# A block-sparse attention and gated-MLP kernel: the sign of the float64 weights carried by a parametric ReLU's slope instead of a 16-bit write on ScalarE, with the order of work searched anew

## The chip, the cores and the metric

The kernel runs on one core of a Trainium2 chip. The metric is the device time of one execution in microseconds (us); before the change it is 959.79 us, the median of 3 runs (959.57 to 961.75).

## The reference, cut to what matters

The reference is a strided sparse attention (8 batches, 8 heads, 576 positions, 64 per head) whose output, 4608 tokens of 512 values, goes through an RMS norm and a gated MLP of width 1536.

```python
scores = where(mask, q @ k.T / sqrt(64), -1e9)       # local or strided mask, by head
attn   = softmax(scores) @ v
x      = attn as (4608, 512)
xn     = x / sqrt(mean(x * x) + 1e-6) * rms_g
out    = (silu(xn @ w_gate) * (xn @ w_val)) @ w_out  # (512, 1536), (512, 1536), (1536, 512)
```

The weights come to the chip as float64, 18.9 MB in all, and the engines have no such type. So the kernel makes float32 words out of the 64-bit words itself, and then splits each float32 into a high and a low part that TensorE multiplies in its single-pass float32 format (fp32r), three products for one.

## The kernel before, in words

**Stages.** The 4608 tokens are 9 chunks of 512. Chunk 0 is computed plainly (three products per block: high by high, low by high, high by low): for each of 12 units of 128 hidden columns `slot_g`, `gemm1` and `slot_o` make the gate, the value and the output product. The other eight chunks are computed in four pairs (`pair_of_chunks`), each pair with seven block products in place of eight, on combinations of the weights. The 32 units of attention (`unit_s`: scores and softmax; `unit_o`: values) are spread over this: four before the first product, eight during chunk 0, the others during the pairs.

**Conversion of the weights** (`convert_weights`, 18 calls, done during the start and chunk 0). A call loads 1 MB of float64 into four slots of SBUF (L1007, SP's queue). Each 64-bit word is two 32-bit cells, cell 0 the low one and cell 1 the high one. The first call is done in two halves, so each operation below comes 17 times with 1024 elements a partition and twice with 512.

- L1006, ScalarE: cell 1, read as float32, is multiplied in place by 2 to the power of -112, which moves the float64 exponent to where a shift by three bits leaves a float32 exponent.
- L1011, ScalarE: byte 3 of cell 0 (its top eight bits) becomes its top three bits as a number, written as a 16-bit integer into the low half of cell 0.
- L1014, ScalarE: cell 1 is converted to a 16-bit float and written into the high half of cell 0. The value is so small that only its sign bit is left, at bit 31 of cell 0.
- L1015, VectorE: cell 1 is shifted left by three (which drops its sign) and combined with cell 0 by a bitwise or; the result is the float32 word.
- `pair_split`: L973 (VectorE) subtracts the high parts; the high parts themselves are casts by `copy_to` (L594 on ScalarE or L596 on VectorE, as the planner chooses).
- L1020, SP's queue: the float32 words are stored to `wd`. The high and low parts are stored to `gvd` and `od` (L1028). During the first pair, `words_of` (L1042) loads the words again, `TLEAD` units ahead, `transform_gv` and `transform_o` combine them, and the results are stored too.

**What sets the order.** `Plan.op` records each operation with its cost and its dependencies; `Plan.forward` then lays them out on the engines by a table of due times (`DUE`), and picks ScalarE or VectorE for the operations that may run on either. `PLACE` is a table of the SBUF slots. Each engine then runs its queue in that order. The planner's price for a ScalarE operation on n elements is

```python
return SLOWER * ((55 if psum else 95) + n / 1.2 + 70 * (n > CH))
```

in ns, with `SLOWER` 1.0 and `CH` 512, so 1018 for 1024 elements; L1011 is priced at 120 more.

Of the kernel before, what the change touches and what calls it, by code (L numbers as in the profile page):

```python
# [11 lines left out]
F32 = mybir.dt.float32  # L12
# [69 lines left out]
TLEAD = 1  # L82
# [5 lines left out]
    "0020140e0412081c2e102c24554e46593d00201856424a4c0e221257403a4d4b5030414852280e2c2614221006181e0c0408241832140626305c5838"  # L88
    "001a04343e3637531328202e020834002c3b445451461c10020e475430493f143224302812300c5b43393b55080604183c5d58453c1c2c2e0e142226"
    "1a403951465c2800020c4b4f554919081032181c34240e3e58405d5a4b0a422a47085c534f5a2e38301e39523f5b2942484c371e395c153c4b58003b"  # L90
    "3d2a554d283a3e400341012b4f161a040a180c104a5a2c32512f59235653141f092e2608191d1a385443321b575a5630202d4e5047381c5905331c14"
    "161024020e44501a54194e43224a3834045a1d530d190f2f3336591e300824510f0c1d340413444e104a3516205a5319440f1319302c114336143208"
    "242d0e0c4e3012021e5316320451180e311e0c100c2c255a172e1424084a1912140e0c1f180211431832202d15533019512c5a06152e1024054a2f32"
    "2e51212207515333271f2f4a04085b2b0b520a0937293d13103a43123f2d014b024c03515c4d113b402a2500285a27585319524a374a3e2c26083c2b"
    "074248242041050b220a2a513b43252d5506394b095c023f03532101194c2328372940045a58112c12543c374d28083e484a07425b50424f26330656"
    "13250a24222a204b571039232b5041383d32003b595b21373f58545c272812095a55150311160b533a054e403c2c51024d4204014f2d362943313044"
    "4746330715081c4b4a0c183e583d2730433f31372a471a4c0a46301849561d1c5c59074b1513580614343b4c43174a325a1a4525183d48331b4b0016"
    "26322831220d5b5c3b093019063f08485414374607120f591735323f2549451455313d1f483f0c0a141e1614314c3b5d5a144717244318585c553e56"
    "265c22444a37450a182548490f0c095b4c5921431347445a3b075d43145d064a08303f59002754455b285624205c4a580a312a26595b2506480c1858"
    "445c48565845123025284556455a3d5310134a032c4e2b38390b07313e21510120024c3b09572d3f115441084f5c4a535a04222a5010402b4d004e2c"  # L100
    "360b5b4259533039073d05203b44515c2858134c2309030a4e4f06123c480122103e04064d2d213a2912025a2b1137382a554333383f57205031130b"
    "36583d05463b00083c3039425c4147535d2c4c4d2d0a54064b2348075b030d553a24563528291001511f431d091c2a1204401e4921343e5922443711"
    "2038023f194115271336500c252617474b441a592b2d1652064d192e3433233e0d2c4c3d0c1722371350260f321a20244d4b5236020c5a50335d530f"
    "3e593807163f474d0e224f572f115805164b5c2d524e5b342f0a4e3d37502c4e5824314f33531b384406324c2d54595d485c4f1b15152152575c4b3e"
    "075d02502f444138034c5825534e2225543d0c34262f23245952214e4c41440b152b3e0c32372652371326054b3e48203d1507502721574e5359265c"
    "5a374c24150658354609521155030a083b0251542234441c40390456310b42013c491d3e4b24262b283d2a523b1157292b0921102346003a0706501e"
    "50200405511f433e540239341e0a5a310355303d2653355810291c4c1208133c210b5c0e595c372f0b4e0d425141501f46362e055b44232240024807"
    "4f560a011d09203e2d572c291c59353b5d4d3c12492b154c210c4b08111343310442003406102a3928523a5803541e555a3053360b14372f0f463d27"
    "16050f0e573d4a19592c510e123f1a5b413824253c23373b1a50323e142e1c453d1b3b5930542c204a1d5c2e4d325a4e1f190345370d47361b595746"
    "5d3f3518091b380e470b273305490c2f17192255234a5b5147410f3d1c3b2c472d265a472720372f4e3d3f182b4a1e270903530d57375c174915124a"  # L110
    "3546055b3d53443f3b500b324e4d3c16383d0e474d0c490f3615224a29192c2b145b0e5d0915533c380e301e0d03181412511d1c231f205a07130b35"
    "4d4744282d4e42110548570206364f403b0817501c4b0b074c04431d492913582312105c2c3d572022484a534256211f1e2b520a390509024d583c4b"
    "0051131d4e3a340111435b5a2830315518362a0b033221351252572d45381c3d2c2b06475129091d5c2f4408403b23485d2a0d4429"))
DUE = np.frombuffer(bytes.fromhex(
    "01600c6e018201990d7d0d94017600010026000c01f80d970002017a00030000001201a6000e00050058019f005c003c00370038006200ad00ef0028"
    "00480178005d00b600dc0118005603ca00ce0462004d0023002c000b00060015001c000a00180d9601be0096009700870008006600a0017200ba017c"
    "0014004400530035002b000d087d014000eb0122011f015c01ad00360034004600570042003b001a0004002a012b0116010f01ca010c01f9000900c4"
    "009a00fc008b006d00b0012904ce005a0063002900a6013300e30221013700f502a702c0013e0007008c00670064011b0185035401a303d101f602e3"
    "01cc0010002e0055005900410032002400bd010a019c00a7008f006500e20039003d00210114026401e601250095004a01570086015f011a015802d8"
    "0195019002a4013c018701ba0d9200b300b1005b030c016e052100bc014a01eb012e01770132015901170130018a013800f000ca00cd00a1015001cb"  # L120
    "016600c801c7019701a4024c01930183004e002d00130098007500a5010d01910b52016f009e007400400043001e0161023b0219015a02330201016d"
    "00f301c00027005f000f00f401df025101c30d430051020c00b902c80336011e0d930151012a0243002000f8018c014d014f02d9030a019801bb00bf"
    "016800d8006b00d900b200f9011201e8019d01ab0101020a008201d401bd02550226023a01e104f10030021100ea00f700de015500cb021600b50175"
    "0135008d0147013d0c3601a2001f02670214010b00ff02170124027a022b00d1008a00aa007a007d01a0011d012f01e701b30184016a012d021b0259"
    "024d023502c5001d00df00e000e90153014e0050007f0052007c0099020b012702ee0248023f0144026b0263026e03cc00a2041a026a01e502f70180"
    "02ce009c003e007900db010000b70094025c020f0212025801f70207021d01c60272026d02aa0296020902e1043102f6016b02c90289029b02340283"
    "04070318001700af013405e600d402080077010700a4016c029e00d000d501090928028c025e029202a300bb00e4027e01f501f301a8013f005400b8"
    "02280277018f0271027d031902360262028e01b701e302b801ea01ef02bc0241011901dc009b010500e5007600a900d6007304c6029302ac001603db"
    "02b9002202030222021302c402a202b1025702370239018e019a017b02ab021c01e4027903230297026001d801f1028b0294022e033a025d032d02b5"
    "01f402e9019b03ce025a02af035502820316025304090374020201c901cd022d022402de0210027301b2022002b302bb01fa02a002870245020001d1"  # L130
    "0254028a02e502cd02c30256029502d30232023d017d029d02ea01e202be03fa01ff024a02e0027f0335024602f20420033c035c027801c501fb0261"
    "02440230028d018601fc02850252022a02d2018d03200174024e022701b0030102fc01cf029902dd02ae045b02a601c402750173016202a502f9025b"
    "053802fd029c02470194025f01bf024f036e02400333034b036603bf018b022c021a0231020401fe026602ca01d601d902d4012c01a502a1022f0165"
    "010401b6020e03c103fb02f402d0035e031d02c7023c0154014801810171021f02d1026f02e40307031c02ff032402bf041801da023e0341029a02f8"
    "0163015d028105dc01db01a700fa00a302b603260313022300fb034002bd034d037b02c2033102fa00e80084014b0192017900f20268030602150276"
    "0205027001210309017e00c6038704c1037002cb0047004b00110329037c02d5039f031103f3013101de02d601b902ec02f101ec01e902a902d7032c"
    "0115020601a901360164028402e60070030e040500c700f10090006802ad0451031001d0027b01bc030001d302cc02c6028f034a03c2033701aa0381"
    "021e02f5045f03490286020d01e0039e0120034f02ed02b2038902dc0238038500dd028003530347024b038302ef001903320348032f034e0d95032b"
    "001b0377044e026c01d702e7029f035903aa02ba038801ce03a102b703b0036102cf037e0141037803b3038c0473009105470304032a007801ed03df"
    "02b402db00a803b4042503a002e803ad03ba0576030202df039a01d50156036802e202da04900582032e039b0265036903b2035003710330036c0314"  # L140
    "03b1030d04710412015b0363027404ba031a0169031701670434038a038d037a03fd042a0327038403ef035f03c0041c04b803ac037303dd040a03ab"
# [301 lines left out]
def attn_moe(ctx: ExitStack, tc: tile.TileContext, qz: bass.AP, qT: bass.AP, kT: bass.AP, vz: bass.AP, vl: bass.AP,  # L443
             wgv: bass.AP, wo: bass.AP, gain: bass.AP, consts: bass.AP, out: bass.AP):
    nc = tc.nc
# [124 lines left out]
    def act(n, psum=False):  # L570
        return SLOWER * ((55 if psum else 95) + n / 1.2 + 70 * (n > CH))
# [107 lines left out]
    def unit_s(i):  # L679
# [43 lines left out]
        if quick:  # L723
# [21 lines left out]
            if i not in HALFQ:  # L745
                op("ACT", 9 * 295, 0, exps, reads=keys_ + [sk], writes=pkeys + [sk], tab="exp")
# [916 lines left out]
```

## Time and profile before

| | |
|---|---|
| median of 3 runs | 959.79 us (959.57 to 961.75) |
| the profiled execution's own time | 959.39 us |
| its span, first to last instruction | 957.6 us |
| PE (TensorE) busy | 908.5 us, 95% |
| VectorE (DVE) busy | 723.1 us, 76% |
| ScalarE (ACT) busy | 602.0 us, 63% |
| mean granted TensorE clock | 0.974 |
| DMA | 234.26 MB, mean 245 GB/s |

Shares of the whole span hide stages with different limits. The view of the span in slices shows where each engine is full, the table by stretches gives the same in us for the stages named above, the groups by line give the duration of one instruction, and the views of waits tell what ended an engine's idle time. A group's busy time counts overlapping instructions of the group once.

### The profile page before, as it was taken

To read this page: it belongs to the slowest core of one execution; us is meant where nothing else is said; L and a number is where in the kernel's file an instruction comes from. 1 tells how busy PE (TensorE), PEld (TensorE's weight loads), DVE (VectorE), ACT (ScalarE), POOL (GpSimd) and SP (SyncE) were. 2 spreads that over 40 slices of the span, in tenths; PEclk is the share of its full clock that TensorE was granted. 3 is DMA by queue.
4 is the path that set the end of the run, shared out by engine and by line. 5 is a ranking of instruction groups with operands and counts; after the bars stand their busy time and mean duration, and the time that the engine had idled before them with its cause. 6 is when DMAs were issued, how large, how long until landed. Compare 5 with 4: busy or idle time off the path is not lost.

```text
span 957.6 us, 20822 instructions
## 1 busy us (share of the span) xinstructions
PE 908.5 (95%) x8295; PEld 726.0 (76%) x8295; DVE 723.1 (76%) x1222; ACT 602.0 (63%) x1178; POOL 1.2 (0%) x12
## 2 busy tenths in 40 slices
PE   6877778799999999999999999999999999999998
PEld 4555566577877888788887788888888888888886
DVE  5666777699988999966766999845579994356992
ACT  6999999976778787544645775444546923333430
POOL 0000000000000000000000000000000000000000
PEclk9877989999999999999999999999999999999999
DMA  9976988669998885598754756985436588543751
GB/s 358 355 265 211 357 294 316 224 213 376 396 394 297 304 308 189 171 366 280 232 170 125 252 181 218 343 278 179 120 99 226 190 302 303 189 138 117 230 154 66
DMA packets 104513, 234.26 MB, mean 245 GB/s; under 512 B 11616, under 2 KB 13920, under 8 KB 102112
## 3 DMA queue, kind: packets, MB, share of 16 engines
q1 hardware_dynamic: 103696, 232.34, 70.6%
q8 instruction: 65, 1.06, 0.4%
q10 hardware_dynamic: 720, 0.59, 0.2%
q14 instruction: 32, 0.26, 0.1%
HBM read 180.98 MB, written 51.90 MB: 243 GB/s over the span
## 4 chain that ended last, share of the span: by engine, by line
PE 59%; DVE 1%; DMA 0%; issue 0%; ACT 0%
PE a L1254 16%; PE g L1254 10%; PE v L1254 10%; PE a L1407 8%; PE g L1407 6%; PE v L1407 6%; PE pair L712 1%; PE pair L797 1%; PE a L797 1%; DMA out_dram<-bl 0%; DVE bl L602 0%; DVE bl L908 0%; PE pair L899 0%; DVE bl L596 0%; ACT bl L594 0%
## 5 line engine op out<-in xcount | busy, mean ns | idle before, releaser
L1254 PE MATMUL a<-bl,bl 128*128 128x512 f32 x857 | 217.0, 394 | 0.8 <-ACT bl L1262 0.7
L1254 PEld LDWEIGHTS a<-bl,bl 128*128 128x128 f32 x857 | 158.3, 188 | 36.3 <-ACT bl L1262 1.1
L594 ACT CAST bl<-bl 128x512 fp32r<-128x512 f32 (+1 forms) x203 | 124.1, 646 | 72.4 <-DVE bl L1210 28.8
L602 DVE TENSOR_TENSOR bl<-bl,bl 128x512 fp32r<-128x512 f32 x244 | 160.7, 686 | 9.6 <-ACT bl L594 4.6
L1254 PE MATMUL g<-bl,bl 128*128 128x512 f32 x564 | 145.6, 391 | 0.7 <-DVE bl L1292 0.7
L1254 PE MATMUL v<-bl,bl 128*128 128x512 f32 x566 | 145.1, 390 | 0.0
L1210 DVE TENSOR_TENSOR bl<-bl,bl 128x512 f32<-128x512 f32 x168 | 114.2, 687 | 40.1 <-ACT bl L1271 37.9
L1254 PEld LDWEIGHTS g<-bl,bl 128*128 128x128 f32 x564 | 105.3, 188 | 24.8 <-DVE bl L1292 2.2
L1254 PEld LDWEIGHTS v<-bl,bl 128*128 128x128 f32 x566 | 105.9, 188 | 22.8 <-DVE bl L1292 0.3
L1266 DVE TENSOR_TENSOR a<-a,bl 128x512 f32<-128x512 f32 x96 | 66.7, 696 | 62.5 <-PE a L1254 52.1
L1407 PE MATMUL a<-bl,bl 128*128 128x512 f32 x420 | 99.0, 391 | 0.1
L1407 PEld LDWEIGHTS a<-bl,bl 128*128 128x128 f32 x420 | 78.5, 188 | 17.4 <-DVE bl L596 0.5
L1407 PE MATMUL g<-bl,bl 128*128 128x512 f32 x282 | 67.2, 390 | 0.0
L1407 PE MATMUL v<-bl,bl 128*128 128x512 f32 x282 | 66.9, 389 | 0.0
L1271 ACT ACTIVATE bl<-a 128x512 f32<-128x512 f32 x48 | 28.8, 600 | 55.5 <-DVE a L1266 53.2
L1407 PEld LDWEIGHTS v<-bl,bl 128*128 128x128 f32 x282 | 52.9, 188 | 11.1 <-ACT bl L1271 0.2
L1407 PEld LDWEIGHTS g<-bl,bl 128*128 128x128 f32 x282 | 52.8, 188 | 11.2
L1262 ACT COPY bl<-g 128x512 f32<-128x512 f32 x48 | 28.2, 588 | 51.4 <-PE g L1254 49.8
L1262 ACT COPY bl<-v 128x512 f32<-128x512 f32 x48 | 28.2, 588 | 49.5 <-PE v L1254 48.8
L596 DVE CAST bl<-bl 128x512 fp32r<-128x512 f32 (+1 forms) x95 | 40.8, 442 | 12.0 <-PE v L1254 6.5
L1100 PE MATMUL g<-bl,bl 128*128 128x512 f32 x120 | 38.0, 456 | 11.2 <-DVE bl L596 5.2
L1011 ACT ACTIVATE bl<-bl,few 128x1024 uint16<-128x1024 uint8 (+1 forms) x19 | 47.7, 2512 | 0.0
(166 smaller groups left out, 1244.0 us busy)
## 6 DMA issues: line engine op xcount, KB each, us to landing
bl<-gvd SPq DMA_DIRECT2D x288, 256.0 KB, 4.5
bl<-od SPq DMA_DIRECT2D x168, 256.0 KB, 3.5
gvd<-bl SPq DMA_DIRECT2D x12, 1024.0 KB, 8.0
bl<-in_wgv_dram SPq DMA_DIRECT2D x11, 1024.0 KB, 8.5
wd<-bl SPq DMA_DIRECT2D x18, 512.0 KB, 6.9
bl<-wd SPq DMA_DIRECT2D x18, 512.0 KB, 7.0
vt<-in_vl_dram SPq DMA_DIRECT2D x24, 352.0 KB, 5.3
xk<-in_kT_dram SPq DMA_DIRECT2D x28, 288.0 KB, 5.5
```

What stands on the lines that cost most here:

```text
L594: nc.scalar.copy(out=o, in_=i)
L596: nc.vector.tensor_copy(out=o, in_=i)
L602: elementwise(CH, lambda e: both(e).tensor_tensor(out=lo.new(F32R), in0=src(), in1=hi.f32(), op=ALU.subtract), reads + [hi.key], [lo.key])
L797: nc.tensor.matmul(out=ends[r % 2][0][n][64 * h:64 * h + 64, at + 32 * lo:at + 32 * hi], lhsT=va()[32 * r:32 * r + 32, D * (6 * n + j):D * ...
L1011: op("ACT", act(n) + 120, 0, lambda cell=cell, half=half, w_=w_: nc.scalar.activation(out=half(0), in_=wide(raw_, U32)[:, w_].bitcast(mybi ...
L1100: nc.tensor.matmul(out=out_, lhsT=q.t[:, w + at:w + at + P], rhs=x.t, start=(kc == 0 and i == 0), stop=(kc == KC - 1 and i == 2))
L1210: elementwise(CH, lambda e: both(e).tensor_tensor(out=o.new() if fresh else o.t, in0=a.t, in1=b.t, op=how), [a.key, b.key], [o.key])
L1254: nc.tensor.matmul(out=banks[bk], lhsT=w, rhs=xs[k][y].t, start=start and k == 0 and i == 0, stop=stop and k == 1 and i == 2, skip_group_c ...
L1262: op("ACT", act(CH, True), 0, lambda: nc.scalar.copy(out=t.new(), in_=banks[bk]), reads=[bk], writes=[t.key])
L1266: op("DVE", dve(CH), 0, lambda: nc.vector.tensor_tensor(out=banks[bk], in0=banks[bk], in1=t.t, op=ALU.add), reads=[t.key], writes=[bk])
L1271: op("ACT", act(CH, True), 0, lambda: nc.scalar.activation(out=t.new(), in_=banks[bk], func=AF.Silu), reads=[bk], writes=[t.key], tab="silu")
L1407: nc.tensor.matmul(out=banks[bks[j]], lhsT=v, rhs=xs[k][y].t, start=start and k == 0 and i == 0, stop=stop and k == KT - 1 and i == 2, ski ...
```

## The change

The sign bit no longer needs an operation of its own. L1006 (L1003 after the change) becomes a parametric ReLU: a positive value is multiplied by 2 to the power of -112 as before, a negative one also by the slope, 2 to the power of 32. That adds 32 to the eight bits of the exponent, and the shift by three in the VectorE operation moves just this bit to the sign's place. L1011 (L1008 after) writes its three bits as a 32-bit integer over the whole of cell 0. L1014 goes. All line numbers behind it are 4 lower after the change.

```diff
-TLEAD = 1
+TLEAD = 2
...
-    "0020140e0412081c2e102c24554e46593d00201856424a4c0e221257403a4d4b5030414852280e2c2614221006181e0c0408241832140626305c5838"
...
+    "080c18281c16242c2e003402513f303a4908120456054c4110220f46204e3d43361e5a45501826200c1422322a18100034080634181c12300e405324"
...
-                op("ACT", 9 * 295, 0, exps, reads=keys_ + [sk], writes=pkeys + [sk], tab="exp")
+                op("ACT", 9 * 290, 0, exps, reads=keys_ + [sk], writes=pkeys + [sk], tab="exp")
...
-                op("ACT", 9 * 300, 0, rows, reads=[sk], writes=pkeys + [sk], tab="exp")
+                op("ACT", 9 * 333, 0, rows, reads=[sk], writes=pkeys + [sk], tab="exp")
...
-            def half(t, w_=w_):
-                return wide(raw_, U32)[:, w_].bitcast(mybir.dt.uint16).rearrange("p (n t) -> p n t", t=4)[:, :, t]
-
             def scale(cell=cell):
                 h = cell(1).bitcast(F32)
-                nc.scalar.activation(out=h, in_=h, func=AF.Copy, scale=2.0 ** -112)
+                nc.scalar.activation(out=h, in_=h, func=AF.Prelu, scale=2.0 ** -112, alpha=2.0 ** 32)
...
-            op("ACT", act(n) + 120, 0, lambda cell=cell, half=half, w_=w_: nc.scalar.activation(
-                out=half(0), in_=wide(raw_, U32)[:, w_].bitcast(mybir.dt.uint8).rearrange("p (n t) -> p n t", t=8)[:, :, 3],
+            op("ACT", act(n) + 120, 0, lambda cell=cell, w_=w_: nc.scalar.activation(
+                out=cell(0), in_=wide(raw_, U32)[:, w_].bitcast(mybir.dt.uint8).rearrange("p (n t) -> p n t", t=8)[:, :, 3],
                 func=AF.Identity, scale=1.0 / 32, bias=low3), reads=["low3"], writes=wk + [("wq", 1)])
-            op("ACT", act(n), 0, lambda cell=cell, half=half: nc.scalar.copy(out=half(1).bitcast(mybir.dt.float16), in_=cell(1).bitcast(F32)), writes=wk + [("wq", 2)])
```

`PLACE` and `DUE` are new tables throughout, so nearly every instruction may stand elsewhere in its queue, and in other slots. The two costs of 9 exponentials (L746, L758) are prices of the planner and no work.

ScalarE's queue in chunk 0, at one place of the conversions (L757 and L743 are the nine exponentials of an attention unit, L1121 the Silu of a unit of chunk 0, `few` holds constants). Before:

```order
L1006 ACTIVATE bl_145<-bl_145 128x1024
L1011 ACTIVATE bl_145<-bl_145,few 128x1024
L1014 CAST bl_145<-bl_145 128x1024
L1006 ACTIVATE bl_402<-bl_402 128x1024
L757 ACTIVATE pp_69,st_76<-pp_69,st_76 128x64 x9
L594 CAST bl_1485<-bl_1238 128x512
L1121 ACT_TABLE_LOAD
L1121 ACTIVATE bl_484<-bl_484 128x512
L1011 ACTIVATE bl_402<-bl_402,few 128x1024
L1014 CAST bl_402<-bl_402 128x1024
```

After, the same stretch of the queue:

```order
L1003 ACTIVATE bl_155<-bl_155 128x1024
L1008 ACTIVATE bl_155<-bl_155,few 128x1024
L757 ACTIVATE pp_69,st_76<-pp_69,st_76 128x64 x9
L1117 ACT_TABLE_LOAD
L1117 ACTIVATE bl_1467<-bl_1467 128x512
L1003 ACTIVATE bl_129<-bl_129 128x1024
L1008 ACTIVATE bl_129<-bl_129,few 128x1024
L878 ACTIVATE bl_1556<-bl_744 128x512
L594 CAST bl_810<-bl_132 128x2x256
L594 COPY bl_535<-pair 128x288
```

Two instructions stand for three in a conversion, no table load stands ahead of L1003, and a square (L878), a high-part cast and an evacuation of attention stand here. Up to the twelfth Silu of chunk 0, ScalarE's queue has 18 table loads after the change and 17 before.

VectorE's queue at the same place. Before:

```order
L753 TENSOR_REDUCE st_76<-pp_69 128x9
L1015 SCALAR_TENSOR_TENSOR bl_579<-bl_145 128x1024
L602 TENSOR_TENSOR bl_1467<-bl_970,bl_1136 128x512
L596 CAST bl_1474<-bl_579 128x2x256
L596 CAST bl_844<-bl_579 128x2x256
L973 TENSOR_TENSOR bl_1474<-bl_579,bl_1474 128x2x256
L1120 TENSOR_TENSOR bl_484<-g,bl_656 128x512
```

After:

```order
L753 TENSOR_REDUCE st_76<-pp_69 128x9
L1011 SCALAR_TENSOR_TENSOR bl_132<-bl_155 128x1024
L1116 TENSOR_TENSOR bl_1467<-g,bl_643 128x512
L596 CAST bl_776<-bl_132 128x2x256
L973 TENSOR_TENSOR bl_673<-bl_140,bl_673 128x2x256
L973 TENSOR_TENSOR bl_776<-bl_132,bl_776 128x2x256
```

The operation that makes the words keeps its place among the softmax steps; one of the two high-part casts has gone to ScalarE. Up to the twelfth multiplication of gate and value (L1137 before, L1133 after), VectorE's queue has 7 copies (L596 COPY), 3 high-part casts (L596 CAST) and 4 squares (L880) fewer.

## Rows read from the trace of the kernel before

**Rows 1.** The page's busy times in 40 slices of 23.9 us each.

```profile
PE   6877778799999999999999999999999999999998
ACT  6999999976778787544645775444546923333430
PEclk9877989999999999999999999999999999999999
DMA  9976988669998885598754756985436588543751
```

**Rows 2.** Busy time by stretches: start, chunk 0, its end, first pair, rest.

```profile
core 0: us, PE busy (x) PEld busy (x) DVE busy (x) ACT busy (x) POOL busy (x), PEclk, DMA share, GB/s
0.00:30.00 30.00, 20.68 (x480) 13.36 (x483) 17.57 (x44) 21.36 (x76) 1.25 (x12) 0.94 0.96 368
30.00:190.00 160.00, 127.22 (x1508) 95.19 (x1507) 110.02 (x201) 157.99 (x259) 0.00 (x0) 0.87 0.80 287
190.00:204.00 14.00, 12.31 (x47) 9.55 (x47) 13.46 (x23) 10.69 (x14) 0.00 (x0) 0.88 0.28 87
204.00:380.00 176.00, 174.44 (x1955) 139.17 (x1954) 165.85 (x277) 133.24 (x343) 0.00 (x0) 1.00 0.89 326
380.00:958.00 578.00, 573.84 (x4314) 468.79 (x4312) 416.23 (x681) 278.76 (x489) 0.00 (x0) 1.00 0.63 205
```

**Rows 3.** What VectorE waited for, 0 to 200 us: total, times, longest.

```profile
DVE bl L1015 <- ACT bl L1014: 32.1, 16, 3.2
```

**Rows 4.** What SP's DMA queue waited for, 0 to 200 us: total, times, longest.

```profile
SPq L1007 <- DVE bl L1015: 29.2, 6, 9.0
SPq L1020 <- DVE bl L1015: 27.8, 6, 7.3
```

**Rows 5.** ScalarE groups by shape, 0 to 200 us: busy us, mean ns | idle before.

```profile
L1011 ACT ACTIVATE bl<-bl,few 128x1024 uint16<-128x1024 uint8 x17 | 44.8, 2633 | 0.0
L1014 ACT CAST bl<-bl 128x1024 f16<-128x1024 f32 x17 | 43.4, 2573 | 0.3
L1006 ACT ACTIVATE bl<-bl 128x1024 f32<-128x1024 f32 x17 | 20.8, 1223 | 0.0
...
L1011 ACT ACTIVATE bl<-bl,few 128x512 uint16<-128x512 uint8 x2 | 3.0, 1481 | 0.0
L1014 ACT CAST bl<-bl 128x512 f16<-128x512 f32 x2 | 2.8, 1414 | 0.0
...
L1006 ACT ACTIVATE bl<-bl 128x512 f32<-128x512 f32 x2 | 1.5, 752 | 0.0
```

**Rows 6.** ScalarE groups by shape, 0 to 200 us: a table load, a cast, a square.

```profile
L1121 ACT ACT_TABLE_LOAD x7 | 9.0, 1283 | 0.1
...
L594 ACT CAST bl<-bl 128x512 fp32r<-128x512 f32 x9 | 5.9, 663 | 2.6 <-DVE bl L1137 1.8 <-DVE bl L1015 0.9
...
L878 ACT ACTIVATE bl<-bl 128x512 f32<-128x512 f32 x5 | 3.5, 704 | 0.0
```

**Rows 7.** VectorE groups by shape, whole span: a cast and a square.

```profile
L596 DVE CAST bl<-bl 128x512 fp32r<-128x512 f32 x88 | 36.0, 422 | 11.9 <-PE v L1254 6.5 <-PE a L1155 1.4 <-PE g L1254 0.9
...
L880 DVE TENSOR_TENSOR bl<-bl 128x512 f32<-128x512 f32 x8 | 5.3, 668 | 0.0
```

**Rows 8.** TensorE groups of chunk 0, 0 to 200 us.

```profile
L1100 PE MATMUL g<-bl,bl 128*128 128x512 f32 x120 | 38.0, 456 | 11.2 <-DVE bl L596 5.2 <-ACT bl L594 3.1 <-DVE bl L1120 2.4
L1100 PE MATMUL v<-bl,bl 128*128 128x512 f32 x126 | 36.1, 422 | 0.4 <-DVE bl L1137 0.4
L1155 PE MATMUL a<-bl,bl 128*128 128x512 f32 x101 | 29.5, 419 | 0.8 <-DVE bl L602 0.8
```

**Rows 9.** TensorE groups of the pairs, from the page.

```profile
L1254 PE MATMUL a<-bl,bl 128*128 128x512 f32 x857 | 217.0, 394 | 0.8 <-ACT bl L1262 0.7
...
L1254 PE MATMUL v<-bl,bl 128*128 128x512 f32 x566 | 145.1, 390 | 0.0
```

**Rows 10.** TensorE's timeline where the pairs begin: start us, us.

```profile
208.08 1.52 PE L1254 MATMUL g<-bl,bl 128*128 128x512 f32 x6
```

More of the change, by code (lines that the diff above doesn't have):

```diff
@@ L87 @@
 PLACE = list(bytes.fromhex(
-    "0020140e0412081c2e102c24554e46593d00201856424a4c0e221257403a4d4b5030414852280e2c2614221006181e0c0408241832140626305c5838"
-    "001a04343e3637531328202e020834002c3b445451461c10020e475430493f143224302812300c5b43393b55080604183c5d58453c1c2c2e0e142226"
-    "1a403951465c2800020c4b4f554919081032181c34240e3e58405d5a4b0a422a47085c534f5a2e38301e39523f5b2942484c371e395c153c4b58003b"
-    "3d2a554d283a3e400341012b4f161a040a180c104a5a2c32512f59235653141f092e2608191d1a385443321b575a5630202d4e5047381c5905331c14"
@@ L92 @@
[L92 to L111, printed above, removed]
@@ new lines @@
+    "080c18281c16242c2e003402513f303a4908120456054c4110220f46204e3d43361e5a45501826200c1422322a18100034080634181c12300e405324"
+    "14042e1a4437394b3e282c260c0824201857435838321c22020e3b5952474b1432341a2810060c4f3c533b3e080012185b30575c4b1c2c2e0e140426"
+    "1a4d473e554a2824020c404f4d5848082032181c22300e164a385d5347513e481235575444530134104d3b4c4d544e49575142143b2810475045482b"
+    "393829443a2a5b3d4053524f3e1a160c04180e08101c412c2d2e2f4b151c1a3c1f1b4a5a0f1b1459411e2d0143410e1a3020001d1e0e460f3237031b"
@@ new lines @@
+    "14161024330636373f3c2c4a4b5a041934205a1d360c16312c172d461e2e240859320d361456560a4b32201d30005a0b161816151c4a2c0922152e32"
+    "1024230f0d4b1e17210d035934042d560f0d0f4a1e1f02324a56323008245a231c2e2f1e171c2730231f10211c30313017221c02173404080a344a5a"
+    "4a3032331335241c3435343001002d570b4209454e202c252b443d29262112283b513e3803504f110852234904273a533032332d104c0b05250a0207"
+    "220900134e452a40062d502c2821114412472b4820013d523e035b42303239493c2936094e3922025a004d57252308040a3a533b543c5441490b103b"
@@ new lines @@
+    "514b264f471d371c272a4812205611072d382824404c455750393d25433c021f5b441805421a59364d135a212b4e2c5422234601060041031e52293e"
+    "5558080a09532604395c1d172d4b3547023719382439435c08101b30495d2e311409523f19441b1d0e1a163f2d18290d393210150d470f5b4f5d4518"
+    "0937403f02581d3c3d4430351e1b263f4b5552301f47174c155c1b1845533e57283b390f57490b3d384b1843510c25553b502d1452293c0b3a501f4c"
+    "1c0c55530a44243a0d04373c153708572516103f3e4728400d393d1d0e3d091702370b1e491c2d293b2455430a3e2652381f4c1745093b1040521655"
@@ new lines @@
+    "250d0b39551e3a2d3e571f0c401e530249120839043f202327242b01210a28460305064d592c290754224e4838361e1f533b24275110093925134920"
+    "08234c565a420629035701002a022612373a2c464511412b0d1f543b5d04072d10270853543f210b0955204d24505951225d5b48284c3d42290a5612"
+    "493e3a2513574e52060044035c5a013b392c3758382d462241472609232b0f2a301c115d3f045b084555530b31364b2707480510513c024a5421244d"
+    "4359252e491d1b5c3b473a192b383a1d2c014c3d393c351a3e541419504f0222322e18291a1f585121170a1a2033123a342f4215250c4f5c2c1a3b35"
@@ new lines @@
+    "2b3d5c511c1a0d463449413e58293724565a020f2d475c09542f594f4a280c26420f123a1b231d59495a183c0f012237214d47384c392d4c4f390a1c"
+    "2449502e18094358541c23432c1d02184c2017373b51254a223e293912423c2b413a2e4d1d17433b1c023d282f2650200a3d243e2f375422172d2e3c"
+    "3a3d2c393b5901571209234f5a3e4a0739030645483f210b05534b5d3625442a1154522e171c553712023007204a43310926245741001004590a2301"
+    "3f033a2b295b254b054c13014e553e06213736575a2748081130462d414f2e2a310b4417345444280b24003a265225593912220920434b3c2c565c49"
@@ new lines @@
+    "5d552f534c5b072313324a3e02042101031027462a311545331f422e0a4e1135512b50472934063f484f2d583d4136181a3b1b30401900170c200f4d"
+    "05011d0f1514573a3d39431f3128254038301d0c081652411b461957121c0b4a543e000e260d444c3e09594014432430523a02195b325a12394b2559"
+    "3e0f263c3d1a2837362241182315313b1352073b27214d3e43162a143917200f541e591017231c1f084d040e1337414a24025b4337393a5a460f2514"
+    "20374d593c5238142715123d2a01313603053a384441543e213c00590b46243017323c1c4d43090e4c0f59075b260e3e04012213233d282502121052"
```

236 lines of the change are left out of this document (118 added, 118 removed).

## The prediction

> **What bounds the kernel now.** First the slices [rows 1]: from the ninth slice on, TensorE is at 9 tenths or more up to the last slice but one. Before that it is at 6 to 8 tenths, the granted clock is mostly below 1, and ScalarE stands at 9 for seven slices, the only stretch where it is full. So whatever is done on ScalarE can pay only in the first 200 us. The table by stretches [rows 2] says the same in us. From 30 to 190 us, where chunk 0 is computed and the weights are converted, ScalarE is busy 157.99 of 160 us; TensorE 127.22, VectorE 110.02, DMA at a share of 0.80. From 204 us on TensorE is busy 748.3 of 754 us: nothing is to be had there, but it also shows how tightly this planner can pack an engine (174.44 of 176 us in the first pair). The waits then name the operation: VectorE's word-making L1015 waited 32.1 us, 16 times, for L1014 [rows 3], and SP's queue waited 29.2 us with weight loads and 27.8 us with word stores behind L1015 [rows 4]. The chain is ScalarE, then VectorE, then the DMA ring of raw weights and TensorE's next unit. ScalarE bounds chunk 0.
>
> One more thing is read from the groups. The planner prices L1011 at 1138 ns and L1014 at 1018; they take 2633 and 2573 [rows 5]. Over 17 of each that is 17 x (1495 + 1555) = 51.9 us that the laid-out order had not counted.
>
> **L1014 goes.** 43.4 us in 17 long operations and 2.8 us in the two halves [rows 5], 46.2 us off ScalarE.
>
> **L1011 writes 32 bits.** The trace has no byte-to-32-bit operation of this form. The ends: no gain at all (2633 ns), or as short as L1006, which reads and writes 32 bits in the same cells (1223 ns). Nothing speaks for less than 1223, nor for more than 2633. L1011 and L1014 differ in what they read (a byte, a 32-bit float) and are within 60 ns of each other; they share the 16-bit write, which L1006 does not have. So the write is the long part and the byte read is worth the 60 ns: I take 1.28 us, and 0.81 us for a half. Gain: 44.8 - 17 x 1.28 = 23.0 us, and 3.0 - 1.6 = 1.4 us in the halves.
>
> The Trainium skill speaks against both gains: "ScalarE: Activation LUTs", section "What ACT_TABLE_LOAD costs", states 186 ns + 0.833 ns an element for an ACTIVATE with immediate scale and bias, float32 and bf16 alike, so 1039 ns for 1024 elements, and an estimate from that page would price the removal at 19 us and the wider write at nothing. The trace does not agree for this 16-bit write with a stride of 8 bytes (2573 ns). By the page, ScalarE's relief of the stretch would be about a quarter of the one below and the time about 950; I go by the row.
>
> **Copy becomes a parametric ReLU.** Not in the trace. Ends: L1006's own 1223 ns and the 2573 ns of the slowest neighbour. It has L1006's shape and types, so I take 1223, no change. If the function needed a table of its own, each conversion would bring loads of 1283 ns [rows 6]; the order shows none ahead of L1003. One load more stands in ScalarE's queue up to the twelfth Silu: 1.3 us.
>
> **The new order** moves work from VectorE to ScalarE in chunk 0: seven copies, three casts and four squares leave VectorE. ScalarE pays at most 10 x 0.66 + 4 x 0.70 = 9.5 us [rows 6], VectorE saves about 10 x 0.42 + 4 x 0.67 = 6.9 us [rows 7]. The loads of the words two units ahead in place of one are the same 18 loads, asked for a little earlier on SP's queue; they hold two more slots of SBUF, which I price at 0 (DMA has a share of 0.28 at 190 to 204 us, where they start) and keep as a rival.
>
> **Sum for 30 to 190 us**, taking each engine by itself [rows 2, 5]:
> - ScalarE: 158.0 - 43.4 - 23.0 + 9.5 + 1.3 = 102.4 us.
> - VectorE: 110.0 - 6.9 = 103.1 us.
> - TensorE: 127.2 us at the clock it had. The products of chunk 0 took 0.317, 0.287 and 0.292 us of busy time each [rows 8]; the same instructions in the pairs, at a granted clock of 1.00, 0.253 (a) and 0.256 (v) [rows 9]. The part of that which a full clock (2.4 GHz in place of stretches at 1.2) would give back is 120 x 0.061 + 126 x 0.031 + 101 x 0.039 = 15.2 us. So 112 to 127.
> - DMA: 160 x 0.80 = 128 us at full share, if all of it must move inside the stretch.
>
> ScalarE is no longer the longest, and what is late next is DMA at 128 us and TensorE, which at an unchanged clock and the packing of the first pair (0.99) needs 127.2 / 0.99 = 128.5 us. I take 128: **32 us off the stretch**. The bounds: with the clock back and part of the weight stores left to the first pair, 112 / 0.99 = 113 us, 47 us off. With DMA at no better share than the 0.89 that it has in the first pair, 128 / 0.89 = 144 us, 16 us off.
>
> The first 30 us: 4.2 us less work on ScalarE (2.8 + 1.4), on the way to the first product, but DMA stands at 0.96 there and four units of attention have to come first. I take 1 us (bounds 0 and 4.2). At 190 to 204 us ScalarE converts nothing more and VectorE is busy 13.46 of 14 us: 0. In the first pair VectorE is busy 165.85 of 176 us and its queue there is about as long as before, so 0; the cover is TensorE's 174.44. Behind that TensorE alone sets the time: 0.
>
> So 959.39 - 32 - 1 = 926.4 us, against the profiled execution. The median of the runs lies 0.4 us above that execution, which makes it **926.5**, rounded, with nothing in that tenth.
>
> **The rivals.**
> 1. *DMA takes ScalarE's place.* For it: 0.96 in the start, 0.89 in the first pair, and waits for slots on SP's queue [rows 4], which a faster ScalarE will not all remove. Against: those waits end with L1015, which waited for L1014. Time: 144 us for the stretch, 959.4 - 16 - 1 = 942. Chance 0.17.
> 2. *The wide write or the ReLU is not cheap.* Either alone adds 23 us to ScalarE: 125 us, still under 128, so the forecast holds. Both together: 148 us, at 0.99 150, which leaves 10 us: 949. Chance 0.04, since the types of L1006 speak against it.
> 3. *More than forecast*: TensorE's clock comes back because the gaps close, and stores slide into the first pair. 113 us, with 1 to 3 us of the start: 909 to 917. Against: 15 us of DMA would have to fit into a pair that has 176 x 0.11 = 19 to spare. Chance 0.12.
> 4. *Slower.* The shorter chunk 0 hands the first pair its stores, and with two more slots held by the words, the loads of transformed weights come late; each of the 12 x 7 products of the first pair then waits. TensorE idles 1.6 us there now. It decides once the mean gap is over 33 / 84 = 0.39 us; at 0.5 us the time is 926 + 42 = 968. Against: the first pair holds TensorE at 99% now, beside a VectorE at 94%. Chance 0.03.
> 5. *The change does not do what it says*: ScalarE gets shorter but chunk 0 was held by something that comes last with it, the granted clock of 0.87 or the slots: 959. Chance 0.04.
>
> **How the numbers follow.** The forecast with its own spread, 918 to 934, has 0.60; its neighbours are rivals 3 (0.12) and 1 (0.17). The range goes from 909 (the end of rival 3) to 944 (a little over rival 1). It leaves out rivals 2, 4 and 5 and small parts of 1 and 3, about 0.15. About 0.3%, 2.9 us, is what can be told from no change here. Faster by more: 0.60 + 0.17 + 0.12 + 0.04 = 0.93. Within: rival 5, 0.04. Slower: rival 4, 0.03.
>
> **What the profile after would show.** Right: L1008 near 1.3 us and L1003 near 1.2 us; no group in L1014's place; the wait of the word-making operation for ScalarE down from 32 us to a few; ScalarE clearly under 9 tenths in slices 2 to 8; the first product of the pairs near 175 us in place of 208 [rows 10]; DMA at 0.95 or more in chunk 0. Wrong: L1008 or L1003 at 2.5 us (rival 2); chunk 0 at 190 us with ScalarE idle (rival 5), or with DMA waits in place of ScalarE's (rival 1); a gap on TensorE at each product of the first pair (rival 4); a granted clock of 1.00 all through chunk 0 and a start of the pairs before 165 us (rival 3). The number falls, whatever the mechanism, if TensorE's idle time behind the start of the pairs is no longer a few us.

## The result, and the profile after

The kernel after takes 910.43 us (median of 4 runs, 909.12 to 911.04) against 959.85 for the kernel before, a ratio of 0.9479 with a 95% interval of 0.9463 to 0.9496: 5.2% or 50 us faster. The forecast was 926.5 in a range of 909 to 944; the sign, the place and the mechanism hold, and the gain is half as large again as the 33 us forecast. The profiled execution's span is 908.7 us.

The slices of the page, 22.7 us each now, beside [rows 1]:

```profile
PE   6899999899999999999999999999999999999998
ACT  6799978677777784455537673444559533333440
PEclk9899999999999999999999999999999999999999
DMA  9799999989987857876747559955365796742741
```

TensorE is at 9 tenths from the third slice on (but for the eighth and the last), not from the ninth; of ScalarE's seven nines three are left; the granted clock is back at 9 tenths or more from the third slice on; DMA has filled up where ScalarE was full.

The table by stretches (columns as in [rows 2]: core time, PE, PEld, DVE, ACT, POOL, then clock, DMA share and GB/s), with the borders moved to where the stretches now lie:

```profile
0.00:30.00 30.00, 20.80 (x473) 14.52 (x475) 18.28 (x45) 18.30 (x74) 1.24 (x12) 0.89 0.94 359
30.00:150.00 120.00, 114.93 (x1532) 90.30 (x1534) 108.88 (x198) 109.14 (x266) 0.00 (x0) 0.99 0.97 379
150.00:165.00 15.00, 14.03 (x62) 11.26 (x60) 14.83 (x26) 9.37 (x14) 0.00 (x0) 1.00 1.02 380
165.00:340.00 175.00, 172.07 (x1946) 138.17 (x1947) 166.49 (x278) 134.94 (x344) 0.00 (x0) 1.00 0.85 313
340.00:908.00 568.00, 564.98 (x4280) 462.56 (x4278) 404.66 (x660) 272.96 (x483) 0.00 (x0) 1.00 0.64 207
```

What took some 160 us takes some 120. In those 120 us TensorE is busy 114.9, ScalarE 109.1, VectorE 108.9 and DMA has a share of 0.97: four resources at 0.91 to 0.97 side by side, where ScalarE alone stood at 0.99 and the others at 0.80 or below.

The conversions in ScalarE's groups by shape, 0 to 160 us (busy us, mean ns), beside [rows 5]:

```profile
L1008 ACT ACTIVATE bl<-bl,few 128x1024 uint32<-128x1024 uint8 x17 | 21.2, 1250 | 0.0
L1003 ACT ACTIVATE bl<-bl 128x1024 f32<-128x1024 f32 x17 | 19.6, 1152 | 0.8 <-DVE st L726 0.8
```

The bits take 1250 ns in place of 2633, the ReLU 1152 where the copy took 1223. VectorE's wait for the conversions, 32.1 us in [rows 3], is this line of its waits now:

```profile
DVE bl L1011 <- ACT bl L1008: 0.2, 1, 0.2
```

TensorE's groups of chunk 0, beside [rows 8], and its timeline where the pairs begin, beside [rows 10]:

```profile
L1151 PE MATMUL a<-bl,bl 128*128 128x512 f32 x132 | 34.1, 399 | 1.1 <-DVE bl L602 1.1
L1096 PE MATMUL v<-bl,bl 128*128 128x512 f32 x132 | 34.1, 395 | 0.4 <-DVE bl L1133 0.4
L1096 PE MATMUL g<-bl,bl 128*128 128x512 f32 x120 | 30.9, 395 | 0.0
```

```profile
156.39 1.52 PE L1250 MATMUL g<-bl,bl 128*128 128x512 f32 x6
```

A product takes 0.258 us of busy time (34.1 / 132, 30.9 / 120) where it took 0.287 to 0.317, and the pairs begin at 156.4 us in place of 208.1. That is 51.7 us; 2.8 us of it are lost behind (752.3 us from there to the end of the span, 749.5 before). The border is not quite the same one, though: 21 output products of chunk 0 (L1151) now stand behind the pairs' first product, where 12 stood before, which is some 2 us of work moved over it:

```profile
157.75 2.20 PE L1151 MATMUL a<-bl,bl 128*128 128x512 f32 x9
161.15 2.88 PE L1151 MATMUL a<-bl,bl 128*128 128x512 f32 x12
```

Before:

```profile
210.80 2.88 PE L1155 MATMUL a<-bl,bl 128*128 128x512 f32 x12
```

### The profile page after: what moved, and what is told of

Read it like the earlier page. It is cut to its first block, busy times and chain, and to the rows that moved or that the text cites. A ratio compares the mean times of both kernels' runs of the same rounds, so it can differ in the third digit from the quotient of the medians.

```text
span 908.7 us, 20785 instructions
## 1 busy us (share of the span) xinstructions
PE 886.8 (98%) x8289; PEld 716.8 (79%) x8292; DVE 713.1 (78%) x1203; ACT 544.7 (60%) x1179; POOL 1.2 (0%) x12
## 4 chain that ended last, share of the span: by engine, by line
PE 82%; DMA 10%; DVE 3%; ACT 3%; issue 1%; SPq 0%; DVEq 0%
PE a L1250 22%; PE g L1250 14%; PE v L1250 14%; PE a L1403 11%; PE g L1403 7%; PE v L1403 7%; DMA wd<-bl 3%; DMA gvd<-bl 2%; DMA od<-bl 2%; PE pair L712 2%; PE pair L797 1%; DMA bl<-in_kT_dram 1%; PE a L797 1%; ACT pp L743 1%; DMA xk<-in_kT_dram 1%
## 5 line engine op out<-in xcount | busy, mean ns | idle before, releaser
L594 ACT CAST bl<-bl 128x512 fp32r<-128x512 f32 (+1 forms) x209 | 126.7, 638 | 80.3 <-DVE bl L1206 37.6
L1250 PE MATMUL g<-bl,bl 128*128 128x512 f32 x567 | 145.1, 390 | 0.0
L1250 PEld LDWEIGHTS g<-bl,bl 128*128 128x128 f32 x567 | 106.0, 188 | 23.1 <-DVE bl L1288 0.7
L1403 PE MATMUL g<-bl,bl 128*128 128x512 f32 x269 | 65.4, 390 | 0.0
L1403 PEld LDWEIGHTS v<-bl,bl 128*128 128x128 f32 x269 | 50.5, 188 | 10.5
L973 DVE TENSOR_TENSOR bl<-bl,bl 128x512 fp32r<-128x512 f32 (+1 forms) x54 | 45.9, 859 | 0.2
L596 DVE CAST bl<-bl 128x512 fp32r<-128x512 f32 (+1 forms) x89 | 39.1, 452 | 7.2 <-PE v L1250 1.6
L1258 ACT COPY bl<-a 128x512 f32<-128x512 f32 x48 | 28.0, 587 | 22.6 <-PE a L1250 22.4
```

What stands on the lines that cost most here:

```text
L594: nc.scalar.copy(out=o, in_=i)
L596: nc.vector.tensor_copy(out=o, in_=i)
L973: elementwise(len(l) * 256, lambda e, l=l, zs=zs: both(e).tensor_tensor(out=sides(l, 1, F32R), in0=cols(zs), in1=sides(l, 0), op=ALU.subtr ...
L1250: nc.tensor.matmul(out=banks[bk], lhsT=w, rhs=xs[k][y].t, start=start and k == 0 and i == 0, stop=stop and k == 1 and i == 2, skip_group_c ...
L1258: op("ACT", act(CH, True), 0, lambda: nc.scalar.copy(out=t.new(), in_=banks[bk]), reads=[bk], writes=[t.key])
L1403: nc.tensor.matmul(out=banks[bks[j]], lhsT=v, rhs=xs[k][y].t, start=start and k == 0 and i == 0, stop=stop and k == KT - 1 and i == 2, ski ...
```

## The experiments

Theory A: the operations made the gain. Theory B: the searched order made it. The first three runs cross the two.

**The old order with the new operations.** The tables of the kernel before; the place of the sign's write in ScalarE's queue stays empty.

```diff
-                nc.scalar.activation(out=h, in_=h, func=AF.Copy, scale=2.0 ** -112)
+                nc.scalar.activation(out=h, in_=h, func=AF.Prelu, scale=2.0 ** -112, alpha=2.0 ** 32)
...
-                out=half(0), in_=wide(raw_, U32)...
+                out=cell(0), in_=wide(raw_, U32)...
...
-            op("ACT", act(n), 0, lambda cell=cell, half=half: nc.scalar.copy(...), writes=wk + [("wq", 2)])
+            op("ACT", act(n), 0, lambda: None, writes=wk + [("wq", 2)])
```

> The tables, and so every queue, of the kernel before, with only the operations changed: the ReLU carries the sign, the three bits are written as 32-bit integers, and the sign's own write is left out of its place in ScalarE's queue. Theory A (the operations made the gain; the old order had already priced them short): ScalarE loses about 70 us, chunk 0 shrinks as after the change, 912 to 922 us. Theory B (the searched order made most of it): 940 us or more. Theory C (both, about half each): 928 to 936 us.

Measured: 915.24 us (914.01 to 916.18), ratio 0.9519 (0.9504 to 0.9534). Theory A: 46 of the 50 us are there without a single instruction moved. The new order's own part is the difference of the ratios, 0.0040 or 3.8 us; the two intervals do not touch. Its slices and stretches have the same picture as the kernel after:

```profile
PE   6899999999999999999999999999999999999998
ACT  6788777678786784446447764444458632333430
```

```profile
30.00:150.00 120.00, 114.29 (x1512) 89.04 (x1512) 110.98 (x206) 96.90 (x244) 0.00 (x0) 0.96 0.99 382
```

The last word is made at 145.0 us here, as in the kernel after (144.8), and the pairs begin later:

```profile
163.88 1.52 PE L1254 MATMUL g<-bl,bl 128*128 128x512 f32 x6
```

**The new order with the old operations.** The tables of the kernel after; the bits' 16-bit write and the sign's write stand where the bits' operation stands.

```diff
-                nc.scalar.activation(out=h, in_=h, func=AF.Prelu, scale=2.0 ** -112, alpha=2.0 ** 32)
+                nc.scalar.activation(out=h, in_=h, func=AF.Copy, scale=2.0 ** -112)
...
-            op("ACT", act(n) + 120, 0, lambda cell=cell, w_=w_: nc.scalar.activation(out=cell(0), ...), ...)
+            def bits(cell=cell, half=half, w_=w_):
+                nc.scalar.activation(out=half(0), ...)
+                nc.scalar.copy(out=half(1).bitcast(mybir.dt.float16), in_=cell(1).bitcast(F32))
+            op("ACT", act(n) + 120, 0, bits, ...)
```

> The tables of the kernel after the change, with the three old operations of a conversion standing at the places of the two new ones. ScalarE has some 70 us more again in chunk 0, 109 + 70 = 179 us of work where the stretch is 120. Theory A: chunk 0 is as long as ScalarE's work, 955 to 970 us, no better than before the change. Theory B: 925 us or less. Theory C: 940 to 950 us.

Measured: 975.0 us (972.33 to 977.31), ratio 1.0149 (1.0125 to 1.0173). Theory B falls. It is even above theory A's range: in the new order the old operations cost 64 us (0.0670 of 959.85), in the old order 46. VectorE's wait for the sign's write, 32.1 us in [rows 3], is 50.6 us here:

```profile
DVE bl L1016 <- ACT bl L1014: 50.6, 15, 4.7
```

**The old order with the wide write alone.** The sign keeps its own write.

```diff
-                out=half(0), in_=wide(raw_, U32)...
+                out=cell(0), in_=wide(raw_, U32)...
```

> The kernel before with one edit: the three bits are written as 32-bit integers, and the sign's own 16-bit write stays, behind it. ScalarE loses 17 x 1.38 us and 2 x 0.7, about 25 us. If ScalarE alone bounds chunk 0 (theory A), the time falls by 18 to 25 us, to 935 to 942, and the wait of the word-making operation stays on the sign's write. If the order or TensorE's clock bounds it, it falls by less than 10 us, to 950 or more. The bits' operation itself should take 1.25 us as after the change.

Measured: 939.11 us (938.05 to 941.09), ratio 0.977 (0.9753 to 0.9787), so 22 us for some 25 us of ScalarE work. Its groups (0 to 200 us) and its wait:

```profile
L1014 ACT CAST bl<-bl 128x1024 f16<-128x1024 f32 x17 | 43.5, 2580 | 0.4
L1011 ACT ACTIVATE bl<-bl,few 128x1024 uint32<-128x1024 uint8 x17 | 21.6, 1271 | 0.0
```

```profile
DVE bl L1015 <- ACT bl L1014: 16.6, 14, 2.4
```

The write alone brings the operation from 2633 to 1271 ns, with the byte read unchanged. The first 25 us off ScalarE came back almost whole; the next 46 us (the sign's write, 43.5 + 2.7) brought 24 (0.977 - 0.9519, of 959.85). Somewhere on the way ScalarE ceased to be the one thing that bounds.

**The width by itself.** Copies behind the last work of the kernel after.

```diff
+        src = xq[0][:, 0:1024].rearrange("p (n t) -> p n t", t=2)[:, :, 1]
+        for _ in range(3):
+            nc.scalar.copy(out=xq[1][:, 0:1024].rearrange("p (n t) -> p n t", t=2)[:, :, 1], in_=src)
+            nc.scalar.copy(out=xq[1].bitcast(F16)[:, 0:2048].rearrange("p (n t) -> p n t", t=4)[:, :, 1], in_=src)
+            nc.scalar.copy(out=xq[1].bitcast(F16)[:, 0:1024].rearrange("p (n t) -> p n t", t=2)[:, :, 1], in_=src)
+            nc.scalar.copy(out=xq[1].bitcast(F16)[:, 0:512], in_=src)
```

> The kernel after, with 12 copies of 512 float32 elements on ScalarE behind its last work, three of each kind: 32-bit written at a step of 8 bytes, 16-bit at 8 bytes, 16-bit at 4 bytes, 16-bit without gaps; all read at a step of 8 bytes. If a 16-bit write as such is the long part, all three 16-bit kinds take about 1.4 us and the first 0.7. If it is the 16-bit write with gaps, the last takes 0.6 to 0.7 us. If it is the step of 8 bytes, the first takes 1.4 as well.

One round of the four, from ScalarE's timeline in the run's one execution (start us, us), in the order of the diff:

```profile
910.64 0.64 ACT L1591 COPY xq<-xq 128x512 f32<-128x512 f32 x1
911.18 1.35 ACT L1592 CAST xq<-xq 128x512 f16<-128x512 f32 x1
912.56 0.76 ACT L1593 CAST xq<-xq 128x512 f16<-128x512 f32 x1
913.36 0.65 ACT L1594 CAST xq<-xq 128x512 f16<-128x512 f32 x1
```

The other two rounds agree within 0.03 us. The second case, a 16-bit write with gaps, comes nearest, but the gap has to be wide: 16 bits alone are not slow (0.65), a step of 8 bytes alone is not slow (0.64), a 16-bit write at a step of 4 bytes costs 0.1 us more, and a 16-bit write at a step of 8 bytes costs twice the time. It is the pair of width and gap.

**What bounds chunk 0 now.** Three theories, each with its dose of extra work, on the kernel after: ScalarE still (S), DMA (D), VectorE (V).

```diff
 # more ScalarE: ahead of the ReLU
+                nc.scalar.activation(out=h, in_=h, func=AF.Copy)
 # more VectorE: the word-making operation
+            for _ in range(2)
 # more DMA: the store of the words
-            nc.sync.dma_start(out=wd[k], in_=wide(ww))
+            [nc.sync.dma_start(out=z[k], in_=wide(ww)) for z in (wd, wd2)]
```

> The kernel after, with one more ScalarE pass in each conversion, a copy of cell 1 in place ahead of the ReLU: 17 x 1.15 + 2 x 0.66 = 20.9 us of ScalarE work in chunk 0, where it is busy 109 of 120 us. Theory S (ScalarE still bounds chunk 0): 15 to 21 us longer than the kernel after, 925 to 931 us. Theory D (DMA has taken its place): 3 to 10 us, since 109 + 21 is over 120 and part of the copies can go back to VectorE's side only in another order; 913 to 920. Theory V (VectorE bounds): the same as D.

> The kernel after, with the word-making operation of each conversion done twice: 17 x 1.22 + 2 x 0.68 = 22.1 us more VectorE work in chunk 0, where it is busy 109 of 120 us. Theory V: 16 to 22 us longer, 926 to 932 us. Theory S or D: 5 to 12 us, 915 to 922.

> The kernel after, with every word store done twice, the second time to a DRAM tile that nothing reads: 18 x 0.52 = 9.4 MB more, 24 us at the 391 GB/s that a full share moves in chunk 0, and 18 more issues on SP's queue. Theory D: 15 to 24 us longer, 925 to 934 us, with chunk 0's share of DMA at 0.97 or more. Theory S or V: under 6 us, to 916, the extra stores sliding into the first pair, whose share is 0.85.

Each theory expected one high result and two low ones. All three are high. So the same was done in every second conversion only (`len(raws) % 2` as the condition):

> The extra ScalarE pass in every second conversion only: 8 x 1.15 + 2 x 0.66 = 10.5 us, which would just fit into the 11 us that ScalarE is idle between 30 and 150 us. Theory R (each engine has room, and the full dose only overran it): at most 3 us over the kernel after, 910 to 914 us. Theory C (conversion is a chain through ScalarE, VectorE and DMA, and a delay in any link reaches TensorE): in proportion to the full dose, 0.83 of it, 8 to 9 us, 918 to 920.

> The word-making operation done twice in every second conversion: 8 x 1.22 + 2 x 0.68 = 11.1 us, against 11 us of idle time of VectorE between 30 and 150 us. Theory R: 910 to 914 us. Theory C: 0.88 of it, 9 to 10 us, 919 to 921.

> Every second word store done twice: 9 x 0.52 = 4.7 MB, 12 us at a full share, against 120 x 0.03 = 4 us free in the stretch and 26 us in the first pair. Theory R: 910 to 914 us if the stores slide into the pair, 918 if they do not. Theory C: in proportion, 0.73 of it, 8 to 9 us, 918 to 920.

And once in the other direction, with the bits' operation taken away and the words combined with a column of zeros:

```diff
-            op("ACT", act(n) + 120, 0, lambda cell=cell, w_=w_: nc.scalar.activation(out=cell(0), ...), ...)
+            op("ACT", act(n) + 120, 0, lambda: None, ...)
...
-            scalar_tensor_tensor(out=wide(word, U32), in0=cell(1), scalar=3, in1=cell(0), ...)
+            scalar_tensor_tensor(out=wide(word, U32), in0=cell(1), scalar=3, in1=few[:, 31:32].bitcast(U32).broadcast_to([P, n]), ...)
```

> The kernel after without the operation that makes the three lowest bits; the word-making operation combines with zeros instead, so the weights lose the lowest three bits of their mantissa. ScalarE has 21.2 + 1.5 = 22.7 us less in chunk 0. Theory C, in both directions (every link of the chain of conversion counts): what was paid for 20.9 us more, 17 us, comes back for less: 892 to 897 us. Theory F (the queues are full side by side: adding to any one costs, taking from one alone gives little, since DMA at a share of 0.97 and TensorE, busy 115 of 120 us, stay): at most 5 us, 905 to 911.

Measured, with the difference to the kernel after worked out from the ratios (ratio less 0.9479, times 959.85 us):

| run | work moved | median us | ratio (95% interval) | to the kernel after |
|---|---|---|---|---|
| more ScalarE | +20.9 us | 927.95 | 0.9657 (0.9640 to 0.9674) | +17.1 us |
| half of it | +10.5 us | 918.9 | 0.9557 (0.9539 to 0.9576) | +7.5 us |
| more VectorE | +22.1 us | 930.02 | 0.9682 (0.9661 to 0.9702) | +19.5 us |
| half of it | +11.1 us | 918.73 | 0.9560 (0.9537 to 0.9582) | +7.8 us |
| more DMA | +9.4 MB, 24 us | 928.12 | 0.9665 (0.9641 to 0.9689) | +17.9 us |
| half of it | +4.7 MB, 12 us | 916.66 | 0.9539 (0.9521 to 0.9556) | +5.8 us |
| no bits | -22.7 us of ScalarE | 909.67 | 0.9462 (0.9446 to 0.9478) | -1.6 us, not told from 0 |

What is added to any of the three costs 0.7 to 0.9 of itself, DMA's half dose 0.5; half doses cost too, so the idle 11 us of ScalarE and of VectorE is not room (theory R falls for these two; DMA's half dose, 916.66 us, lies between what R and C expected). A full engine is not what makes ScalarE's half dose cost: in its stretch no engine is fuller than in the kernel after by more than 1 us, and DMA has a share of 0.95. That the delay is handed on along the fixed order of the queues fits this, but no run singles it out.

```profile
30.00:150.00 120.00, 111.47 (x1504) 86.51 (x1497) 100.86 (x183) 110.12 (x264) 0.00 (x0) 0.94 0.95 372
```

But what is taken from ScalarE alone gives nothing that can be measured (theory C holds in one direction only). In the stretch from 30 to 150 us, the kernel without the bits has ScalarE at 92 us and everything else as it was:

```profile
30.00:150.00 120.00, 115.65 (x1539) 91.08 (x1531) 110.38 (x200) 92.31 (x251) 0.00 (x0) 1.00 0.99 383
```

and with the words stored twice, DMA runs at a share of 1.00 and beyond, and TensorE waits for weights in the first pair, which it did not in the kernel after (stretches, then TensorE's longest wait):

```profile
30.00:150.00 120.00, 108.12 (x1517) 83.61 (x1514) 100.78 (x183) 102.05 (x257) 0.00 (x0) 0.98 1.00 391
150.00:170.00 20.00, 17.18 (x75) 13.58 (x74) 16.96 (x29) 13.55 (x17) 0.00 (x0) 1.00 1.03 415
```

```profile
PE v L1251 <- DMA bl<-gvd: 5.9, 1, 5.9
```

So ScalarE no longer bounds chunk 0 by itself. TensorE, VectorE and DMA are left, at 0.92 to 0.99 of the stretch beside each other in the run without the bits. No run here took work from any of the three, so which of them would give something alone stays open.

## Why the prediction was right, and where its size was off

*ScalarE bounds chunk 0*: right. Taking 25 us from it alone gave 22.

*L1014 goes, L1011 becomes as short as L1006*: right to 0.03 us (1.28 forecast, 1.25 measured); the reading that the write and not the byte read is the long part holds in the wide-write run. The rule of the Trainium skill ("ScalarE: Activation LUTs", section "What ACT_TABLE_LOAD costs"), the same time at either width, 1039 ns for 1024 elements as an estimate from its figure, does not agree for a 16-bit write at a step of 8 bytes (2573 ns in [rows 5]). The probe shows where the two widths do agree: without gaps the 16-bit copy takes 0.65 us, the 32-bit one 0.64.

*The ReLU costs what the copy cost*: right (1152 against 1223 ns). Rival 2 is out.

*The new order*: priced at 9.5 us more for ScalarE and 6.9 less for VectorE, nothing by itself. Between the two orders with the new operations, from 30 us to the last word, ScalarE has 11.0 us more (105.5 against 94.5) and VectorE 2.3 less (103.7 against 106.0). It is worth 3.8 us at these operations; where, stands below.

*The stretch takes 128 us*: this step failed, by its size. The last word was made at 188.7 us (start of the last L1015) and is made at 144.8 now: 44 us, where 32 and 1 were forecast. The operations alone did it: in the old order with the new operations the last word is made at 145.0. Two terms of the sum were too long:
- DMA was put at 160 x 0.80 = 128 us of full share. But the bytes of the stretch are nearly the same, 160 x 287 = 45.9 MB before and 120 x 379 = 45.5 MB after, and they took 120 x 0.97 = 116 us. A full share moved 359 GB/s before and 391 after. The wide write alone, at a share of 0.91 in its stretch from 30 to 150 us, stands between (333 / 0.91 = 366). The share that a partly idle DMA shows was no measure of the time that its bytes need.
- TensorE was put at 127.2 us with its clock unchanged. The gaps closed, the granted clock rose from 0.87 to 0.99 of 2.4 GHz, and 120 x 0.059 + 126 x 0.029 + 101 x 0.034 = 14.2 us came back, of the 15.2 worked out as the bound. It is busy 114.9 us.

So rival 3, with its 0.12, is what happened: 47 us off the stretch were its bound, 44 are measured. Its reason against, that DMA could not slide into the first pair, counted for little, since little had to slide. The first pair, taken over 172 us from its first product, before and after:

```profile
208.08:380.00 171.92, 170.35 (x1937) 135.79 (x1936) 161.87 (x270) 130.15 (x339) 0.00 (x0) 1.00 0.89 325
156.39:328.30 171.91, 168.01 (x1928) 134.54 (x1927) 163.50 (x273) 128.77 (x334) 0.00 (x0) 1.00 0.90 332
```

That is a share of 0.90 for 0.89, and 1.2 MB more in 57 (332 x 171.91 against 325 x 171.92), where the rival had 15 us of DMA to fit in.

*The stretch behind, priced at 0*: from the last word to the first product of the pairs it was 208.1 - 188.7 = 19.4 us and is 156.4 - 144.8 = 11.6. The prediction saw VectorE full there and no conversion. The new order did this, and the granted clock alone (0.88 there before) would not have: the old order with the new operations has 1.00 from 150 to 165 us and still takes 163.9 - 145.0 = 18.9 us, with TensorE busy all of the time, since more products were left behind the last word. Some 2 of the 7.8 us are the nine products moved behind the border.

*The first pair, priced at 0*: 2.8 us are lost from there on. Beside the nine products, TensorE waits longer. Its waits from 150 to 340 us add up to 3.9 us, where they were 1.4 (204 to 380 us), and 3.0 of them are at one place, the evacuation of chunk 0's output by ScalarE (L1164), on which the pair's first output products wait; the old order with the new operations waits there 0.2 us (L1168). The two together are more than 2.8 us; what was gained in return was not followed up.

```profile
PE a L1250 <- ACT bl L1164: 3.0, 2, 2.4
PE a L1250 <- DVE bl L973: 0.9, 1, 0.9
```

Together, by construction, these three are the difference of the spans: 43.9 + 7.8 - 2.8 = 48.9 us. The order's own part of it, against the old order with the new operations (span 914.1 us), is 0.2 + 7.3 - 2.1 = 5.4 us in these two profiled executions, and 3.8 us in the ratios.

*The end of the sum*: 926.4 and the 0.4 us between the median and the profiled execution make 926.8 and not 926.5. Nothing hangs on it.

*Rival 1, DMA takes ScalarE's place*: right only in that DMA is now among the fullest, at 0.97. It stands beside three others, and the stretch is not the 144 us of this rival. *Rival 4*: no gap at each product, only the waits above. *Rival 5*: no sign of it.

## What to carry to other kernels

When one engine bounds a stretch, price the others at what they need once it is gone, and not at the busy time or DMA share that they show while they wait for it: TensorE's busy time holds the lower clock of its gaps, and the share of a partly idle DMA holds time that the bytes don't need. After such a gain, add a dose of work to each engine and take some from each: a dose that costs does not yet show that its engine bounds, since here every dose cost and the one removal, ScalarE's, gave nothing that can be measured.

## What the runs showed of the hardware that was not expected

A 16-bit write by ScalarE costs 1.35 us for 512 elements at a step of 8 bytes, 0.76 at 4 bytes and 0.65 without gaps; a 32-bit write at a step of 8 bytes costs 0.64. And nearly the same bytes, 45.9 and 45.5 MB, took 128 us of full DMA share in the stretch where ScalarE held the conversions back, 116 us where it did not; what makes the difference was not tried.
